# The expert part's GpSimd sums given to VectorE, two more rows fetched ahead of the optional slots, and the last operands moved behind a guard

## The chip, the cores and the metric

The kernel runs on one core of one Trainium2 chip, as one launch. The metric is the device time of a run in microseconds (us); the time before is the median of three runs. The engines are named as the profile names them: PE is TensorE's matmul, PEld its weight load, DVE is VectorE, ACT is ScalarE, POOL is GpSimd, SP is SyncE. An engine with a "q" behind it (ACTq, POOLq) is that engine's instruction queue: branches, semaphore work and DMA issues.

## The reference, cut to what matters

```
attn_out = attention(x, state)              # 8 batches
x = rearranged to 4352 tokens of 512        # 34 tiles of 128 tokens
e_idx = argmax(x @ w_gate)                  # one of 8 experts a token
for e in range(8):
    mask = e_idx == e
    h = maximum(x[mask] @ w1[e], 0)         # 512 -> 1024
    out[mask] = gate_w[mask] * eom[mask, e] * (h @ w2[e])
h = out @ w_in                              # 512 -> 2048, float64 weights
g = h * clip(h + 3, 0, 6) / 6
result = g @ w_out                          # 2048 -> 512, float64 weights
```

## The kernel before, in words

Every fp32 product is made of three: each operand is kept as a high part (a copy rounded to the type fp32r, cast by ACT) and a low part (the subtraction, on DVE or POOL), and PE adds high·high, low·high and high·low. So whatever PE multiplies has first passed ACT and then a subtraction.

The program has three stretches. Until about 107 us of the span it computes the attention and the routing. Then comes the **expert part** (functions `early` and `moe1`, to about 614 us). The tokens, sorted by expert, are dealt to 41 slots of 128 rows; where an expert's last slot isn't full it is padded, so the number of slots that hold tokens depends on the data. Slots 19 to 25 are optional (`OPT`): all work of such a slot stands behind a guard (`guard`, L1299 in the profile), a branch on a register that every engine takes for itself. In this run slots 19 to 22 are computed and 23 to 25 skipped. Last comes the second part (`moe2`, from 614 us), six blocks of eight `unit`s each, matmuls of 384 columns and their activations.

What slot t does: `gather` fetches its 128 rows by an indirect DMA on POOL's queue, after `column` has fetched their row numbers (`ci`); `slot_T` transposes them on PE and splits them (`xh` by ACT, `xl` by DVE); `slot_M1` is 24 matmuls of 512 columns against the first weights `w00h`/`w00l` in the order xh·w00h, xl·w00h, xh·w00l for each half of the columns, with the relu on ACT; `slot_TH` transposes the result and splits it (`hh` by ACT, `hl` by DVE); `slot_M2` is 24 matmuls against `w01h`/`w01l` in the order hh·w01h, hl·w01h, hh·w01l; ACT scales the result and it is stored in `ys_dram`.

The loop of `moe1` orders them in iteration t as: column t+5, gather t+3, M1 of t, T of t+1, `weights` of t+1 for the first matrix, one or two conversion pieces, M2 of t-1, TH of t, `weights` of t for the second matrix. Three helpers in it matter here.

- `weights` (L735): when a flag of slot t says that a new expert begins, four pieces of 128x1024 are split: ACT casts the high part (L703), and the low part (L709) is subtracted by DVE in pieces 0, 2 and 3 and by POOL in piece 1. Behind the branch SP fetches the raw weights of the expert after that (L726) into the tile that was just split.
- `convert` (32 pieces in iterations 2 to 18 and 26 to 36, two of them in 29, 31, 33 and 35) turns float64 words of the second part's weights into fp32: seven DVE operations (L924 to L931) and one POOL addition (L933, tile `quad`). `parts` then splits them (tile `st`, L944 on ACT, L945 on DVE) and SP writes them to DRAM.
- The rows of slot 26 (`OPT.stop`), the first one behind the optional slots, are fetched and transposed early, in iterations 13 and 14 (`HOIST`), into tiles of their own.

At the seam between expert part and second part, iteration 40 also builds the operands `X` of the second part's first block (`block_operands`, seven steps `ops[0]` to `ops[6]`; the splits are L1044 on ACT and L1045 on DVE, two sums L1053 on DVE). The last slot's M2 isn't done in the loop: `last_M2` (L1070) cuts it into three parts of 8 matmuls, which stand in the gaps of the first `unit`, behind its first two products (L1116, 12 matmuls), its third and fourth, and its fifth.

The expert part is laid out by a schedule that is fixed when the program is built: each engine has one list of instructions and works through it in order, with waits on semaphores ("waits Pool_49" is a wait on POOL's counter).

Of the kernel before, what the change touches and what calls it, by code (L numbers as in the profile page):

```python
# [9 lines left out]
F32 = mybir.dt.float32  # L10
# [4 lines left out]
ALU = mybir.AluOpType  # L15
# [5 lines left out]
P = 128  # L21
B, H, S, NS, D = 8, 8, 512, 32, 64
NT = B * (S + NS)
DM = H * D
# [3 lines left out]
OPT = range(19, 19 + SLOTS - TILES)  # L28
# [667 lines left out]
def split(k, which, i, eng):  # L696
    high(k, which, i)
    low(k, which, i, eng)


def high(k, which, i, copy=None):
    c = slice(1024 * i, 1024 * i + 1024)
    (copy or k.nc.scalar.copy)(k.W[0][which][0][:, c], k.raw[which].rearrange("p a b -> p (a b)")[:, c])  # L703


def low(k, which, i, eng):
    hi, lo = k.W[0][which]
    c = slice(1024 * i, 1024 * i + 1024)
    eng.tensor_tensor(out=lo[:, c], in0=k.raw[which].rearrange("p a b -> p (a b)")[:, c], in1=hi[:, c], op=ALU.subtract)  # L709
# [8 lines left out]
def fetch(k, t, which):  # L718

    nc = k.nc  # L720
    raw, queue = k.raw[which], nc.sync
    if t not in k.lregs:
        fetch_flags(k, t)
    nd, ev = k.lregs[t]
    src = (k.w1_d, k.w2_d)[which]
    queue.dma_start(out=raw, in_=src[bass.ds(ev, 1)].rearrange("o (k p) f -> p (o k) f", p=P), cond=nd)  # L726


def weights(k, t, which):
    if t == SLOTS:  # L730
        return
    if t not in k.regs:
        k.regs[t] = k.nc.values_load(k.tab[0:1, 0, t:t + 1], engines=[ET.Activation, ET.DVE, ET.Pool], min_val=0,
                                     max_val=1)
    with k.tc.If(k.regs[t] == 1):  # L735
        for i in range(4):
            split(k, which, i, k.nc.gpsimd if i == 1 else k.nc.vector)
    if t < SLOTS - 1:
        fetch(k, t, which)

# [9 lines left out]
def guard(k, t):  # L750
    if t not in OPT or t in k.inside:
        return nullcontext()
    return k.tc.If(k.vregs[t] == 1)


def column(k, t):
    if t >= SLOTS or t in k.ci:
        return
    nc = k.nc
    queue, engine = (nc.sync, ET.SP) if t < EARLY + 5 else (nc.gpsimd, ET.Pool)  # L760
    col = nc.values_load(k.cols[0:1, t:t + 1], engines=[engine], min_val=0, max_val=511)
    own = "o" * (t == OPT.stop)
    ci = k.tb.tile([P, 4], I32, tag="ci" + own, name="ci", bufs=1 if own else 8)
    queue.dma_start(out=ci, in_=k.inv_d.rearrange("(p c) o -> p c o", p=P)[:, bass.ds(col, 1), :].rearrange("p c o -> p (c o)"))
    k.ci[t] = ci


def gather(k, t):
    if t >= SLOTS or t in k.xg or t in k.xT:
        return  # L770
    x = k.xgp.tile([P, DM + 1], F32, tag="xg", name="xg", bufs=4)
    ins = k.nc.gpsimd.indirect_dma_start(
        out=x[:, 0:DM], out_offset=None, in_=k.xs[0:P * EARLY_TILES] if t < EARLY else k.xs,
        in_offset=bass.IndirectOffsetOnAxis(ap=k.ci[t][:, 0:1], axis=0))
    if t < EARLY:
        k.tc.keep_in_program_order(ins)
    k.xg[t] = x
# [125 lines left out]
def convert_load(k, i):  # L903
    if i >= NCONV:
        return
    r, c = convert_place(i)
    d = k.cv.tile([P, CW, 2], I32, tag="d", name="d", bufs=2)
    src = (k.win_d if i < NCONV // 2 else k.wout_d).bitcast(I32)
    k.nc.gpsimd.dma_start(out=d.rearrange("p a b -> p (a b)"), in_=src[r:r + P, 2 * c:2 * c + 2 * CW])
    k.cvd[i] = d  # L910


def convert(k, i):
    if i >= NCONV:
        return
    nc = k.nc
    v = nc.vector
    d = k.cvd.pop(i)
    if i % 4 == 0:
        k.quad = k.cv.tile([P, 4, CW], F32, tag="quad", name="quad", bufs=2)  # L920
    hw, lw = d[:, :, 1], d[:, :, 0]
    e = k.wk.tile([P, 2, CW], I32, tag="e", name="e", bufs=1)[:, 0]
    base = float(896 << 20)
    v.tensor_scalar(out=e, in0=hw, scalar1=0x7FF00000, scalar2=None, op0=ALU.bitwise_and)  # L924
    v.tensor_scalar(out=e, in0=e, scalar1=base, scalar2=float(1151 << 20), op0=ALU.max, op1=ALU.min)
    v.tensor_scalar(out=e, in0=e, scalar1=base, scalar2=8.0, op0=ALU.subtract, op1=ALU.mult)
    v.scalar_tensor_tensor(out=e, in0=hw, scalar=-0x80000000, in1=e, op0=ALU.bitwise_and, op1=ALU.bitwise_or)
    v.tensor_scalar(out=hw, in0=hw, scalar1=3, scalar2=0x7FFFF8, op0=ALU.logical_shift_left, op1=ALU.bitwise_and)
    v.tensor_tensor(out=hw, in0=hw, in1=e, op=ALU.bitwise_or)
    f = e.bitcast(F32)  # L930
    v.scalar_tensor_tensor(out=f, in0=lw.bitcast(mybir.dt.uint32), scalar=2.0 ** -52, in1=f, op0=ALU.mult, op1=ALU.mult)  # L931
    w = k.quad[:, i % 4, :]
    nc.gpsimd.tensor_tensor(out=w, in0=f, in1=hw.bitcast(F32), op=ALU.add)  # L933
    if i >= NCONV // 2:
        k.tasks.append(lambda f=i - NCONV // 2: out_part(k, f, w))
    elif i % 4 == 3:
        k.tasks += in_sums(k, i // 4, k.quad)
# [11 lines left out]
def out_part(k, f, w):  # L949

    st = parts(k, w, (2, CW))
    k.nc.sync.dma_start(out=k.wdn[f], in_=st.rearrange("p h c -> p (h c)"))
# [314 lines left out]


FLAGS, HOIST = -6, OPT.start - 6
PIECES = sorted([t for t in range(2, 37) if t not in OPT] + [29, 31, 33, 35])  # L1270


def moe1(k):
    k.tasks = []
    k.cv = k.xb = k.tc.alloc_tile_pool(name="conv", bufs=1, reuse_waits="tile")
    convert_load(k, 0)
    convert_load(k, 1)
    i = 0

    def piece(n=2):  # L1280
        nonlocal i
        for _ in range(min(n, len(k.tasks))):
            k.tasks.pop(0)()
        convert(k, i)
        convert_load(k, i + 2)
        i += 1

    for t in range(2, SLOTS):
        if t - FLAGS in [*OPT, OPT.stop]:
            flags(k, t - FLAGS)  # L1290
        if t == OPT.start:
            k.fixed = {}
        if t == HOIST:
            column(k, OPT.stop)
            gather(k, OPT.stop)
        column(k, t + 5)
        gather(k, t + 3)
        within = t in OPT and t - 1 in OPT
        with guard(k, t - 1) if within else nullcontext():  # L1299
            if within:  # L1300
                k.inside = (t - 1,)
            if t > EARLY:
                start_y(k, t - 1)
            slot_M1(k, t)
            if t + 1 < SLOTS and t + 1 != OPT.stop:
                slot_T(k, t + 1)
            if t == 39:
                for j in (2, 3):
                    block_T(k, k.blocks[0], j, ("y2", "y3")[j % 2])
            if t == 38:  # L1310
                for j in (0, 1):
                    block_T(k, k.blocks[0], j, ("y2", "y3")[j % 2])
                for j in (2, 3, 4):
                    block_gather(k, k.blocks[0], j)
            if t == 40:
                fetch_down(k, 0, 0)
                for f in ops[0:3]:
                    f()
            weights(k, t + 1, 0)
            if t == 39:  # L1320
                k.ring.fetch()
            for _ in range(PIECES.count(t)):
                piece()
            if t == PIECES[-1] + 1:
                piece(6)
            if t > EARLY:
                slot_M2(k, t - 1)
            if t == 39:
                block_gather(k, k.blocks[0], 5)
                block_T(k, k.blocks[0], 4, "y2")  # L1330
            if t == 40:
                ops[3]()
            slot_TH(k, t)
            if t == 40:
                for f in ops[4:]:
                    f()
            if t == 39:
                block_T(k, k.blocks[0], 5, "y3")
                ops = block_operands(k, k.blocks[0])
            if t == HOIST + 1:  # L1340
                slot_T(k, OPT.stop)
            weights(k, t, 1)
        k.inside = ()
        if t + 1 == OPT.stop:
            k.fixed = None
        if 4 <= t < 11:
            row_table(k, 5 * (t - 4))
        if t == 37:
            assert i >= NCONV and not k.tasks
            k.cv.release()  # L1350
            k.reg = k.tc.alloc_tile_pool(name="region", bufs=1, reuse_waits="tile")
            k.blocks = [Block(k, g) for g in range(len(HALVES))]
            k.ring = Ring(k, 8 * len(k.blocks))
            for j in (0, 1):
                block_gather(k, k.blocks[0], j)
        if t == 40:
            k.ring.fetch()
# [84 lines left out]
```

## Time and profile before

| | us |
|---|---|
| median of three runs | 1372.44 (1371.67 to 1373.47) |
| the profiled execution | 1371.76 |
| its span | 1370.2 |
| PE busy in the span | 1319.0 (96%) |
| DVE, ACT, POOL busy | 796.7 (58%), 564.5 (41%), 286.1 (21%) |
| granted TensorE clock, mean | 0.985 of full speed |

The span runs from the profiled execution's first instruction to its last; its time is 1.56 us longer. All places below are given in us from the span's start. In a timeline an entry can stand for several instructions of one kind (the x behind it), its us run from the first one's start to the last one's end, and in brackets stands how long the engine was idle before it and what released it. "issue" is a wait that nothing in the profile explains.

### The profile page before, as it was taken

Reading aid. Unit: us, or ns where it says so; the run is one execution under the profiler, and the core shown is the slowest. Engines: PE = TensorE matmul, PEld = TensorE weight load, DVE = VectorE, ACT = ScalarE, POOL = GpSimd, SP = SyncE. Lnnn points to the kernel's source line nnn. Section 1 sums busy time; section 2 is a strip of 40 time slices with the busy share of each in tenths; the row PEclk is TensorE's granted clock in tenths of the full one; section 3 lists DMA queues with packets and bytes.
Section 4 is the critical chain, followed back from the end, with each engine's and each line's share of the span. In section 5 each row is a group of like instructions: output and inputs, shape, how many; then the busy total and the mean of one; then the engine's idle time right before and its main releaser. Section 6 shows DMA issues by size and latency. Waiting matters only on the chain.

```text
span 1370.2 us, 20252 instructions
## 1 busy us (share of the span) xinstructions
PE 1319.0 (96%) x7091; PEld 1119.1 (82%) x7091; DVE 796.7 (58%) x1525; ACT 564.5 (41%) x1021; POOL 286.1 (21%) x290
## 2 busy tenths in 40 slices
PE   8977999999997999998999999999999999999996
PEld 6766888888775788877989898889898988888885
DVE  7987588877725776435446445644564465445442
ACT  5753344453533433343334433443353344333432
POOL 2346333343423343210000200020010001000101
PEclk9999999999998999999999999999999999999998
DMA  9964768867642554346553433353333334333540
GB/s 352 362 207 141 237 211 266 253 197 233 223 158 94 201 172 160 125 161 231 207 205 110 169 123 123 111 182 146 138 138 147 124 115 156 123 135 117 200 169 32
DMA packets 84289, 238.22 MB, mean 174 GB/s; under 512 B 9104, under 2 KB 24592, under 8 KB 84048
## 3 DMA queue, kind: packets, MB, share of 16 engines
q1 hardware_dynamic: 56896, 168.46, 35.1%
q0 software_dynamic: 15824, 46.57, 10.7%
q10 hardware_dynamic: 11456, 21.78, 4.3%
q8 instruction: 58, 0.95, 0.3%
q14 instruction: 55, 0.45, 0.1%
HBM read 312.98 MB, written 54.09 MB: 268 GB/s over the span
## 4 chain that ended last, share of the span: by engine, by line
PE 47%; issue 6%; ACT 1%; DVE 0%; POOL 0%; POOLq 0%; ACTq 0%
PE ch L1116 22%; PE acc L1087 8%; PE acc L1089 8%; PE acc L1088 8%; PE xTp L1030 1%; PE yp L1070 0%; POOL out_dram L1101 0%; ACT o L1100 0%; DVE r L1132 0%; ACT g L1136 0%; ACT r L1128 0%; DVE g L1139 0%; POOLq L1429 0%; DVE s L1169 0%; DVE s L1183 0%
## 5 line engine op out<-in xcount | busy, mean ns | idle before, releaser
L1116 PE MATMUL ch<-X,wr 128*128 128x384 f32 (+1 forms) x2016 | 367.8, 329 | 0.8 <-DVE oid L1027 0.8
L1116 PEld LDWEIGHTS ch<-X,wr 128*128 128x128 f32 x2016 | 342.5, 188 | 20.7 <-DVE s L1183 2.4
L1139 DVE TENSOR_TENSOR g<-r,g 128x384 fp32r<-128x384 f32 (+1 forms) x192 | 103.0, 537 | 84.7 <-ACT g L1136 79.1
L1136 ACT CAST g<-r 128x384 fp32r<-128x384 f32 (+1 forms) x192 | 95.1, 495 | 135.2 <-DVE r L1132 104.5
L1128 ACT ACTIVATE r<-s,three 128x384 f32<-128x384 f32 (+1 forms) x144 | 86.4, 600 | 139.5 <-DVE s L1169 115.5
L1132 DVE SCALAR_TENSOR_TENSOR r<-r,s 128x384 f32<-128x384 f32 (+1 forms) x144 | 77.3, 537 | 73.0 <-ACT r L1128 71.8
L1101 POOL DMA_INDIRECT out_dram<-o,oid x34 | 33.5, 986 | 382.3 <-ACT o L1100 374.3
L1014 POOL DMA_INDIRECT xg<-ys_dram,rowi x34 | 39.1, 1151 | 340.9 <-DVE oid L1027 250.7
L1087 PE MATMUL acc<-w01h,g 128*128 128x512 f32 x272 | 110.1, 405 | 0.0
L1087 PE MATMUL acc<-w00h,g 128*128 128x512 f32 x272 | 107.7, 396 | 0.7 <-ACT o L1100 0.7
L1089 PE MATMUL acc<-w00h,g 128*128 128x512 f32 x272 | 108.1, 397 | 0.0
L1088 PE MATMUL acc<-w00l,g 128*128 128x512 f32 x272 | 107.3, 394 | 0.0
L1089 PE MATMUL acc<-w01h,g 128*128 128x512 f32 x272 | 107.2, 394 | 0.0
L1088 PE MATMUL acc<-w01l,g 128*128 128x512 f32 x272 | 107.2, 394 | 0.0
L1132 DVE SCALAR_TENSOR_TENSOR r<-r,ch 128x384 f32<-128x384 f32 (+1 forms) x48 | 25.6, 532 | 120.5 <-ACT r L1128 120.5
L834 ACT ACTIVATE h<-hp 128x512 f32<-128x512 f32 x76 | 45.0, 599 | 121.8 <-PE hp L802 119.1
L802 PE MATMUL hp<-w00h,xh 128*128 128x512 f32 x304 | 90.0, 418 | 5.0 <-ACTq L1299 2.0
L802 PE MATMUL hp<-w00l,xh 128*128 128x512 f32 x304 | 86.3, 404 | 6.8 <-POOL w00l L709 4.9
L1128 ACT ACTIVATE r<-ch,three 128x384 f32<-128x384 f32 (+1 forms) x48 | 27.1, 564 | 154.2 <-PE ch L1116 154.2
L802 PE MATMUL hp<-w00h,xl 128*128 128x512 f32 x304 | 85.9, 406 | 0.0
L802 PE MATMUL yp<-w01h,hh 128*128 128x512 f32 x296 | 78.4, 406 | 1.4 <-ACTq L735 1.0
L802 PEld LDWEIGHTS hp<-w00l,xh 128*128 128x128 f32 x304 | 58.1, 192 | 23.1 <-POOL w00l L709 5.7
(224 smaller groups left out, 2251.0 us busy)
## 6 DMA issues: line engine op xcount, KB each, us to landing
raw<-in_w_dram SPq DMA_DIRECT2D x75, 2048.0 KB
wr<-wup_dram SPq DMA_DIRECT2D x48, 1792.0 KB
wup_dram<-st SPq DMA_DIRECT2D x28, 512.0 KB
ys_dram<-y ACTq DMA_DIRECT2D x41, 256.5 KB
xt<-in_xt_dram SPq DMA_DIRECT2D x8, 1040.0 KB
xT<-in_xT_dram SPq DMA_DIRECT2D x16, 512.0 KB
xs_dram<-row ACTq DMA_DIRECT2D x8, 1024.0 KB
d<-in_win_dram POOLq DMA_DIRECT2D x16, 512.0 KB, 5.4
```

Of the source, the lines that this page charges most:

```text
L802: nc.tensor.matmul(out, a, b, start=(i == 0), stop=(i == len(parts) - 1))
L834: nc.scalar.activation(h[:, 512 * f:512 * f + 512], ps[f], AF.Relu)
L1014: k.nc.gpsimd.indirect_dma_start(out=x, out_offset=None, in_=k.ys[0:P * min(T + 8, SLOTS)], in_offset=bass.IndirectOffsetOnAxis(ap=k.rowi[ ...
L1087: nc.tensor.matmul(a, g[:, 0, t], wh[:, c], start=not late and u == 0, stop=False)
L1088: nc.tensor.matmul(a, g[:, 0, t], wl[:, c], start=False, stop=False)
L1089: nc.tensor.matmul(a, g[:, 1, t], wh[:, c], start=False, stop=bool(late) and u == 7)
L1101: ins = nc.gpsimd.indirect_dma_start(out=k.out, out_offset=bass.IndirectOffsetOnAxis(ap=b.ids[j], axis=0), in_=o, in_offset=None).ins
L1116: nc.tensor.matmul(ps[:, 0:W], w[:, d, i, hw, :], b.X[i][:, hx, d, :], start=start and n == 0, stop=n == 5, skip_group_check=True)
L1128: nc.scalar.activation(rs[kind], h, AF.Relu, bias=k.three)
L1132: v.scalar_tensor_tensor(out=rs[kind], in0=rs[kind], scalar=6.0, in1=h, op0=ALU.min, op1=ALU.mult)
L1136: nc.scalar.copy(k.gs[kind][:, 0], rs[kind])
L1139: v.tensor_tensor(out=k.gs[kind][:, 1], in0=rs[kind], in1=k.gs[kind][:, 0], op=ALU.subtract)
```

## The change

- `weights`: the subtraction of piece 1 goes from POOL to DVE.
- `convert`: the last addition goes from POOL to DVE.
- `HOISTS`: slots 27 and 28 get their row numbers and rows early too, in iterations 14 and 15, in tiles of their own (`xgo27`, `xgo28`). Their transposes stay where they were.
- Iteration 40: `ops[4:]`, which are the split of X[3], the two sums and the splits of X[4] and X[2], are emitted behind `weights(k, 40, 1)` instead of ahead of it. The flag of slot 40 is not set in this run.

```diff
@@ def weights(k, t, which):
     with k.tc.If(k.regs[t] == 1):
         for i in range(4):
-            split(k, which, i, k.nc.gpsimd if i == 1 else k.nc.vector)
+            split(k, which, i, k.nc.vector)
@@ def column(k, t):
-    own = "o" * (t == OPT.stop)
+    own = f"o{t}" if t in HOISTS else ""
     ci = k.tb.tile([P, 4], I32, tag="ci" + own, name="ci", bufs=1 if own else 8)
@@ def gather(k, t):
-    x = k.xgp.tile([P, DM + 1], F32, tag="xg", name="xg", bufs=4)
+    if t in HOISTS[1:]:
+        x = k.cv.tile([P, DM], F32, tag=f"xgo{t}", name="xg", bufs=1)
+    else:
+        x = k.xgp.tile([P, DM + 1], F32, tag="xg", name="xg", bufs=4)
@@ def convert(k, i):
     w = k.quad[:, i % 4, :]
-    nc.gpsimd.tensor_tensor(out=w, in0=f, in1=hw.bitcast(F32), op=ALU.add)
+    v.tensor_tensor(out=w, in0=f, in1=hw.bitcast(F32), op=ALU.add)
@@
+HOISTS = [OPT.stop, OPT.stop + 1, OPT.stop + 2]
@@ def moe1(k):
-        if t == HOIST:
-            column(k, OPT.stop)
-            gather(k, OPT.stop)
+        if HOIST <= t < HOIST + 3:
+            column(k, HOISTS[t - HOIST])
+            gather(k, HOISTS[t - HOIST])
@@
             slot_TH(k, t)
-            if t == 40:
-                for f in ops[4:]:
-                    f()
             if t == 39:
                 block_T(k, k.blocks[0], 5, "y3")
                 ops = block_operands(k, k.blocks[0])
             if t == HOIST + 1:
                 slot_T(k, OPT.stop)
             weights(k, t, 1)
+            if t == 40:
+                for f in ops[4:]:
+                    f()
```

Line numbers of the changed kernel are 3 higher than before around L709 to L930 and 4 higher from L1299 on; the name of a row tells it in any case.

**Place 1** is PE's list where the skipped optional slots end and slot 26's M1 begins (`w00l` is the low part of the first weights). Before:

```order
L1299 UNCONDITIONAL_BRANCH
L1299 UNCONDITIONAL_BRANCH [waits PE_49]
L802 MATMUL hp<-w00h,xh 128x512 [waits Activation_49] x4
L802 MATMUL hp<-w00h,xl 128x512 x4
L802 MATMUL hp<-w00l,xh 128x512 [waits DVE_49]
L802 MATMUL hp<-w00l,xh 128x512 [waits Pool_49]
L802 MATMUL hp<-w00l,xh 128x512 [waits DVE_49] x2
L802 MATMUL hp<-w00h,xh 128x512 x4
```

Changed:

```order
L1303 UNCONDITIONAL_BRANCH
L1303 UNCONDITIONAL_BRANCH [waits PE_49]
L805 MATMUL hp<-w00h,xh 128x512 [waits Activation_49] x4
L805 MATMUL hp<-w00h,xl 128x512 x4
L805 MATMUL hp<-w00l,xh 128x512 [waits DVE_49] x4
L805 MATMUL hp<-w00h,xh 128x512 x4
```

The wait on POOL's counter is gone; all four low pieces are waited for on DVE's.

**Place 2** is DVE's list at the first conversion, with the split of the hidden values (`hl`) behind it. Before:

```order
L929 TENSOR_TENSOR d<-d,e 128x512 [waits DVE_49]
L931 SCALAR_TENSOR_TENSOR e<-d,e 128x512 [waits DVE_49]
L853 TENSOR_TENSOR hl<-tp,hh 128x512 [waits Activation_49] x2
L735 COMPARE_AND_BRANCH
L709 TENSOR_TENSOR w01l<-raw_67,w01h 128x1024 [waits DMAHW1_49,Activation_49]
L709 TENSOR_TENSOR w01l<-raw_67,w01h 128x1024 [waits Activation_49] x2
```

Changed:

```order
L932 TENSOR_TENSOR d<-d,e 128x512 [waits DVE_49]
L934 SCALAR_TENSOR_TENSOR e<-d,e 128x512 [waits DVE_49]
L936 TENSOR_TENSOR quad<-e,d 128x512 [waits DMAHW3_49,DMAHW2_49,DVE_49]
L856 TENSOR_TENSOR hl<-tp,hh 128x512 [waits Activation_49] x2
L735 COMPARE_AND_BRANCH
L709 TENSOR_TENSOR w01l<-raw_67,w01h 128x1024 [waits DMAHW1_49,Activation_49]
L709 TENSOR_TENSOR w01l<-raw_67,w01h 128x1024 [waits Activation_49] x3
```

The addition stands between the last integer operation and `hl`, and a split of weights has four DVE pieces in a row instead of three.

**Place 3** is DVE's list at the seam to the second part, from the last slot's `hl` on (`X` are operands of the first block, `s_8388` the sum of the unit's second product, `r` and `ch` belong to its first activation). Before:

```order
L853 TENSOR_TENSOR hl<-tp,hh 128x512 [waits Activation_49] x2
L1045 TENSOR_TENSOR X<-xraw,X 128x768 [waits DMAHW1_49,Activation_49]
L1053 TENSOR_TENSOR xraw<-xraw,s_8256 128x2x384 [waits DVE_49] x2
L1156 TENSOR_TENSOR s_8388<-ch,s_8387 128x384 [waits DMAHW0_49,PE_49,Activation_49]
L1045 TENSOR_TENSOR X<-xraw,X 128x768 [waits DMAHW0_49,Activation_49]
L1045 TENSOR_TENSOR X<-xraw,X 128x768 [waits DMAHW4_49,Activation_49]
L735 COMPARE_AND_BRANCH
```

Changed:

```order
L856 TENSOR_TENSOR hl<-tp,hh 128x512 [waits Activation_49] x2
L735 COMPARE_AND_BRANCH
L709 TENSOR_TENSOR w01l<-raw_67,w01h 128x1024 [waits DMAHW0_49,Activation_49]
L709 TENSOR_TENSOR w01l<-raw_67,w01h 128x1024 [waits Activation_49] x3
L735 UNCONDITIONAL_BRANCH
L735 UNCONDITIONAL_BRANCH [waits DVE_49]
L1159 TENSOR_TENSOR s_8388<-ch,s_8387 128x384 [waits DMAHW0_49,PE_49,Activation_49]
L1048 TENSOR_TENSOR X<-xraw,X 128x768 [waits DMAHW1_49,Activation_49]
L1056 TENSOR_TENSOR xraw<-xraw,s_8256 128x2x384 [waits DVE_49] x2
L1135 SCALAR_TENSOR_TENSOR r<-r,ch 128x384 [waits Activation_49]
L1048 TENSOR_TENSOR X<-xraw,X 128x768 [waits DMAHW0_49,Activation_49]
L1048 TENSOR_TENSOR X<-xraw,X 128x768 [waits DMAHW4_49,Activation_49]
```

The guard stands directly behind `hl` now, the unit's sum comes ahead of the X splits, and one step of the activation (L1135) stands among them. ACT's list changes in the same way: the copy of the unit's first product comes directly ahead of the guard, and the casts of X[3], X[4] and X[2] behind it.

## Rows read from the trace of the kernel before

**Rows 1.** The page, part 1: busy us, share of the span, instructions of each engine.

```profile
PE 1319.0 (96%) x7091; PEld 1119.1 (82%) x7091; DVE 796.7 (58%) x1525; ACT 564.5 (41%) x1021; POOL 286.1 (21%) x290
```

**Rows 2.** Windows: stretch, its us, busy of PE, PEld, DVE, ACT, POOL, granted clock, DMA share, GB/s.

```profile
140.00:630.00 490.00, 471.86 (x2220) 381.97 (x2219) 316.76 (x528) 203.30 (x324) 165.00 (x174) 0.98 0.58 190
415.00:425.00 10.00, 7.99 (x18) 5.83 (x19) 0.15 (x1) 0.60 (x1) 3.33 (x6) 0.50 0.21 56
```

**Rows 3.** Waits, all engines: who waited for whom, us in total, times, longest.

```profile
PE yp L1070 <- ACTq L735: 5.6, 1, 5.6
PE hp L802 <- POOL w00l L709: 4.9, 2, 2.9
...
PE yp L802 <- DVE hl L853: 0.9, 1, 0.9
```

**Rows 4.** Timeline, 360 to 370 us, DVE and PE.

```profile
362.87 3.51 DVE L709 TENSOR_TENSOR w00l<-raw,w00h 128x1024 fp32r<-128x1024 f32 x3
...
368.66 0.97 PE L802 MATMUL hp<-w00l,xh 128*128 128x512 f32 x3 [2.00 <-POOL w00l L709]
```

**Rows 5.** Timeline, 412 to 430 us, PE at slot 26's first product.

```profile
415.58 1.22 PE L802 MATMUL hp<-w00h,xh 128*128 128x512 f32 x2 [1.09 <-issue]
...
420.36 1.65 PE L802 MATMUL hp<-w00l,xh 128*128 128x512 f32 x3 [1.43 <-POOLq L1299]
...
426.11 0.60 PE L815 MATMUL xTp<-ident,xg 128*128 128x128 f32 x4
```

**Rows 6.** Timeline, 440 to 452 us, slot 27's first product.

```profile
442.33 0.39 PE L802 MATMUL hp<-w00l,xh 128*128 128x512 f32 x1
442.76 3.31 DVE L927 SCALAR_TENSOR_TENSOR e<-d,e 128x512 int32<-128x512 int32 x1
443.17 2.35 POOL L709 TENSOR_TENSOR w00l<-raw,w00h 128x1024 fp32r<-128x1024 f32 x1
...
445.57 1.65 PE L802 MATMUL hp<-w00l,xh 128*128 128x512 f32 x3 [2.86 <-POOL w00l L709]
...
447.91 1.28 DVE L853 TENSOR_TENSOR hl<-tp,hh 128x512 fp32r<-128x512 f32 x2
...
450.73 0.60 PE L815 MATMUL xTp<-ident,xg 128*128 128x128 f32 x4
```

**Rows 7.** Timeline, 612 to 635 us, the seam to the second part.

```profile
615.00 1.28 DVE L853 TENSOR_TENSOR hl<-tp,hh 128x512 fp32r<-128x512 f32 x2
615.56 0.49 ACT L1154 COPY s<-ch 128x384 f32<-128x384 f32 x1
...
618.05 1.70 ACT L1044 CAST X<-xraw 128x768 fp32r<-128x768 f32 x2 [2.00 <-DVE xraw L1053]
...
619.27 1.81 DVE L1045 TENSOR_TENSOR X<-xraw,X 128x768 fp32r<-128x768 f32 x2
...
619.85 3.59 PE L1070 MATMUL yp<-w01h,hh 128*128 128x512 f32 x8 [5.60 <-ACTq L735]
...
625.39 2.03 PE L1070 MATMUL yp<-w01l,hh 128*128 128x512 f32 x8
...
627.26 2.27 PE L1116 MATMUL ch<-X,wr 128*128 128x384 f32 x12
```

**Rows 8.** Line L709: durations of one in ns (min/median/max), first and last start, forms.

```profile
L709 DVE TENSOR_TENSOR w00l<-raw,w00h x21: 1210/1220/4050, 95.5 to 439.0; 128x1024 fp32r<-128x1024 f32 x21
...
L709 POOL TENSOR_TENSOR w00l<-raw,w00h x7: 2352/2458/2500, 93.7 to 443.2; 128x1024 fp32r<-128x1024 f32 x7
```

**Rows 9.** Lines, DVE by form: count, busy us, mean ns of one, idle before.

```profile
L1132 DVE SCALAR_TENSOR_TENSOR r<-r,s 128x384 f32<-128x384 f32 x120 | 67.0, 559 | 62.1 <-ACT r L1128 61.1
L929 DVE TENSOR_TENSOR d<-d,e 128x512 int32<-128x512 int32 x32 | 22.2, 693 | 1.1
```

**Rows 10.** Timeline, 154 to 161 us, the tightest conversion.

```profile
156.44 1.28 DVE L853 TENSOR_TENSOR hl<-tp,hh 128x512 fp32r<-128x512 f32 x2
...
157.18 1.69 PEld L802 LDWEIGHTS yp<-w01h,hl 128*128 128x128 f32 x8 [0.51 <-DVE hl L853]
```

## The prediction

> **What bounds the kernel now.** I read the page's busy shares first, then the list of waits, then the timeline around each wait that ended PE's idle time. PE is busy for 96% of the span [rows 1], so a change of the other engines can win only what PE idles, and what its lower clock costs behind a pause. In the 490 us from 140 to 630 us, the stretch in which the change acts, PE is busy 471.86 us; 18.1 us is all its idle time. DVE is busy 316.76 us there, 65%, and POOL 165.00 [rows 2]. The waits say where the 18.1 us lie: 5.6 us in one piece at the seam, where PE waits for ACT to pass the guard L735, and 4.9 us in two pieces, where PE waits for POOL's low piece of the weights [rows 3]. The timelines add 1.43 us on POOL's way past the skipped slots [rows 5], and what a pause does to the clock: the stretch 415 to 425 us shows the granted clock at 0.50, that is 1.2 of 2.4 GHz [rows 2]. A row of eight 512-column matmuls takes 625.39 to 627.26, which is 0.234 us each at full clock, and 3.59 us, 0.45 each, behind the wait at 619.85 [rows 7].
>
> **The change part by part.** *(a) Weights at 366 us.* PE came to its low matmuls at 366.66 and waited 2.00 us, to 368.66, for POOL's piece [rows 4]. A DVE piece is 1.22 us by the median, a POOL piece 2.46 [rows 8]; three DVE pieces take 3.51 us [rows 4], so 1.15 of pitch, and four end at 362.87 + 4 x 1.15 + 0.06 = 367.53. PE, unstopped from 366.66, wants the fourth at 366.66 + 2 x 0.234 = 367.13. It waits 0.40 in place of 2.00: **gain 1.6** (1.2 to 2.4; below if the pieces run a third slower, above if the next raw weights, which load when the last subtraction is done, arrive earlier).
>
> *(b) Slot 26 behind the skipped slots.* The wait of 1.43 on POOL goes [rows 5]; DVE's count is reached, since the neighbouring piece of DVE let PE through before POOL did. From 415.58 to 426.11 PE does 22 matmuls in 10.53 us [rows 5], at full clock 22 x 0.234 = 5.15. So the gain lies between 1.43 (clock stays low) and 5.38 (full at once). The wait marked "issue", 1.09, ahead of it stays [rows 5], so part of the low clock has a cause that is not removed: I take the middle, **3.4**.
>
> *(c) Slot 27.* PE's first low matmul ends at 442.33 + 0.39 = 442.72; it waits 2.86 for POOL's piece, and the remaining 15 matmuls end at 450.73, 8.01 us later, in place of 15 x 0.234 = 3.51 [rows 6]. **Gain 4.5** (2.86 to 4.6). While POOL subtracts, DVE's L927 takes 3.31 us [rows 6], though its neighbour of the same size, L929, has a mean of 0.693 [rows 9]; without POOL's piece that 2.6 us is back, which pays for DVE's fourth piece (1.15) and the addition (0.69). DVE's `hl`, at 447.91 before [rows 6], comes about 0.8 earlier, PE 4.5 earlier; it still lies ahead of its use, barely.
>
> The other ten POOL pieces ended no wait of PE [rows 3]; DVE's work instead of them is paid for in the same way, since a DVE piece at its side is held too (maximum 4.05 against a median of 1.22 [rows 8]). I cost them at nothing; if that cover failed, each could cost up to 1.15.
>
> *(d) The additions.* 32 more DVE operations of 0.69 (the nearest row is L929, same size [rows 9]) make 22 us, in DVE's idle 35%. Each stands ahead of `hl`. The first is the tightest: `hl` was late already, PE's weight load waited 0.51 for it at 157.18 [rows 10], so it loses 0.7. In the others that I followed in the timeline, `hl` is done before PE turns to it, mostly by more than 0.69. The one place where PE waited 0.9 for `hl` [rows 3] lies behind an iteration in which DVE itself waited for POOL's addition, which took longer than DVE's will; it gets shorter by some 0.3. **Loss 0.4** (0 to 4, the upper end being six such places at 0.69).
>
> *(e) The seam.* Before, PE waited 5.60 us, from 614.25 to 619.85, because ACT had to cast X[4] and X[2] (ended 618.05 + 1.70 = 619.75) ahead of the guard [rows 7]. Changed, ACT's copy of the unit's first product is the last thing ahead of it. It ended at 615.56 + 0.49 = 616.05 behind a cast of X[3]; without that cast I put it at 615.4, and the guard at 0.1 (619.75 to 619.85). PE then does 8 matmuls (1.87), two products (623.28 to 625.39, 2.11), 8 more (1.87) [rows 7]: 615.5 + 5.85 = 621.35. Now DVE comes last: `hl` ends at 615.00 + 1.28 = 616.28, and from there to 619.27 + 1.81 = 621.08 six operations took 4.8 us [rows 7]. Changed: 616.28 + 0.2 for the guard (twice ACT's) + 4.8 + 0.56 for the activation's step, which now stands among them (L1132 [rows 9]), + 0.56 for the sum behind it = 622.4. The next pair of products starts there instead of at 627.26: **gain 4.8**. Ends: 5.9, if DVE is not what PE waits for (621.35); 2.3, if a guard costs 1.09 (the "issue" row [rows 5]) and the two casts' 1.70 lie in series with DVE: 616.28 + 1.09 + 4.8 + 1.12 + 1.70 = 625.0.
>
> For a branch a row shows 0.1 (ACT, 619.85) and up to 1.09 (PE, 415.58). The Trainium skill (Runtime: NRT & Kernel Launch, Instruction fetch mechanics) says that a taken branch to a target outside the loaded window has to fetch its instructions before execution goes on; by that rule the seam's guard, which is jumped over in this run, would cost nearer to 1.09 on DVE, and the gain of (e) would be 3.9, towards R1 below. No row shows such a fetch there.
>
> *The hoist.* The rows of slots 27 and 28 ended no wait of PE; the early fetches are two more short issues on POOL's queue in a stretch where nothing waits for POOL. **0**.
>
> Sum: 1.6 + 3.4 + 4.5 - 0.4 + 4.8 = **13.9 us**. Against the profiled execution's 1371.76 that is 1357.9; the median of the runs is 0.68 higher, so **1358.5**.
>
> **The rivals.** *R1, a new wait at the seam:* the moved operands come later than PE wants them, and the gain of (e) is 2.3, not 4.8: 1361.0. For it: six DVE operations and two casts pile up behind one guard; against: DVE stands idle afterwards. *R2, the skipped slots keep PE slow:* another engine's way past the guards takes POOL's place, (b) gives nothing: 1361.9; both together 1364.4. For it: PE waits for ACT and for "issue" right before.
>
> *R3, slower: VectorE becomes the one that ends last.* Every `hl` comes 0.69 late and PE waits for it: 32 x 0.69 = 22.1 us lost against the 14.3 of (a), (b), (c) and (e), that is 1372.44 + 7.8 = 1380.2. It decides when `hl` has less than 0.69 us to spare in over 24 of the 32 conversions ((14.3 + 2.7) / 0.69). For it: the row at 157.18; against: DVE's 65%, and POOL no longer holds it. The Trainium skill speaks for this rival (Perfetto Trace Analysis, Optimizing Scalar/DVE Operations): it would move work away from a saturated DVE, to GpSimd too, though it adds that the two share a read port of SBUF. At 65% the trace does not show saturation.
>
> *R4, no change:* each removed wait is replaced by one on DVE's piece as long: 1372.4.
>
> **How the numbers follow.** Forecast 0.62, R1 0.17, R2 0.11, R3 0.06, R4 0.04. A measurement tells 0.2%, 2.7 us, from no change; so faster 0.90 (forecast, R1, R2), same 0.04 (R4), slower 0.06 (R3). The ends: all low values give 1.2 + 1.4 + 2.9 + 2.3 - 4 = 3.8, that is 1368.6; all high ones 2.4 + 5.4 + 4.6 + 5.9 = 18.3, that is 1354.1, and the 0.9 us at `hl` and a tenth at each of the ten swaps that I cost at nothing, whose raw weights load earlier, could go too: 1352.2. That all are low at once is unlikely: the range is **1352 to 1367**, which takes in the forecast, R1 and R2 with most of their bounds and leaves out R3 and R4.
>
> **What would show it.** Right: no wait of PE on POOL's `w00l`; slot 26's M1 shorter by about 3 us; PE's last M2 at the seam starting 1 to 1.5 us after the TH, and its next pair of products near 622.4 less what was won before it; DVE near 68 to 70% in the stretch. Wrong: PE's waits on `hl` growing from 0.9 us to 5 or more (d, R3), a wait of PE on DVE's X or sum at the seam of over 3 us (R1), the clock between slots 25 and 27 as low as before (R2).

## The result and the profile after

The changed kernel takes 1355.49 us (median of four, 1352.62 to 1358.56) against 1372.06 for the kernel before beside it: ratio 0.9878, 95% interval [0.9849, 0.9907], 16.6 us less at the medians. The forecast was 1358.5 in a range of 1352 to 1367. The profiled execution took 1357.82 us, 13.9 less than that of before; it lies in the upper half of the four runs. Two executions at a far lower granted clock, one of the kernel before (2418 us at 0.82) and one with the hoist put back (2163 us at 0.56), are left out of every comparison below.

The page, part 1, of the changed kernel, and the two windows that answer to [rows 2] (the same columns; the first ends at 617 us, since the seam comes earlier):

```profile
PE 1314.4 (97%) x7091; PEld 1117.6 (82%) x7091; DVE 809.7 (60%) x1569; ACT 564.2 (42%) x1021; POOL 211.0 (16%) x246
```

```profile
140.00:617.00 477.00, 465.26 (x2215) 377.56 (x2214) 329.51 (x571) 202.47 (x324) 92.41 (x130) 0.99 0.61 196
413.50:423.50 10.00, 8.01 (x28) 5.99 (x28) 0.15 (x1) 0.91 (x2) 2.00 (x4) 0.83 0.10 31
```

DVE's busy share of the stretch went from 65 to 69% (329.51 of 477), and PE's idle time in it from 18.1 us to 11.7 (477 - 465.26). In the ten us at slot 26 PE did 28 matmuls in place of 18, at a granted clock of 0.83 in place of 0.50; but the two windows do not lie alike to the start of the slot. From the slot's first matmul to the transposes behind it, before and changed, the windows are:

```profile
413.76:426.11 12.35, 9.83 (x24) 6.95 (x25) 0.15 (x1) 0.60 (x1) 4.61 (x6) 0.59 0.24 67
414.26:422.99 8.73, 7.49 (x24) 5.63 (x25) 0.15 (x1) 0.60 (x1) 1.23 (x3) 0.80 0.11 33
```

So the slot's first product is 3.6 us shorter, at a clock of 0.80 in place of 0.59.

PE's longest waits in the changed kernel from 140 to 640 us (who waited for whom, us in total, times, longest):

```profile
PE yp L805 <- ACT w01h L703: 2.9, 3, 2.5
PE hp L805 <- ACTq L1303: 2.0, 1, 2.0
PE yp L805 <- DVE hl L856: 1.9, 2, 1.6
PE hp L805 <- issue: 1.2, 1, 1.2
PE yp L1073 <- ACTq L735: 1.2, 1, 1.2
PE ch L1119 <- DVE s L1166: 1.0, 1, 1.0
```

The two largest waits of before [rows 3] are gone or small: none on POOL's pieces is left, and 1.2 us of 5.6 at the seam. But the first row, PE's wait of 2.9 us for the cast of `w01h`, was 0.2 us before.

To see where the time went, take PE instructions that both kernels have and compare their starts. Timeline of the changed kernel, PE, at such places:

```profile
361.89 1.31 PE L805 MATMUL hp<-w00h,xh 128*128 128x512 f32 x4
...
363.98 1.41 PE L805 MATMUL hp<-w00l,xh 128*128 128x512 f32 x4
...
368.03 0.60 PE L818 MATMUL xTp<-ident,xg 128*128 128x128 f32 x4
...
380.52 0.60 PE L818 MATMUL xTp<-ident,xg 128*128 128x128 f32 x4
...
383.57 0.73 PE L805 MATMUL yp<-w01h,hh 128*128 128x512 f32 x2 [2.46 <-ACT w01h L703]
...
387.44 2.81 PE L805 MATMUL yp<-w01h,hl 128*128 128x512 f32 x8
...
416.23 1.04 PE L805 MATMUL hp<-w00h,xh 128*128 128x512 f32 x2 [1.24 <-issue]
...
422.99 0.60 PE L818 MATMUL xTp<-ident,xg 128*128 128x128 f32 x4
...
442.28 1.10 PE L805 MATMUL hp<-w00l,xh 128*128 128x512 f32 x4
...
443.22 0.60 PE L818 MATMUL xTp<-ident,xg 128*128 128x128 f32 x4
...
614.92 2.35 PE L1119 MATMUL ch<-X,wr 128*128 128x384 f32 x12 [1.02 <-DVE s L1166]
```

The same instructions of before started at these times (four of them are not in the rows above the prediction):

```profile
363.88 0.94 PE L802 MATMUL hp<-w00h,xh 128*128 128x512 f32 x3
...
372.28 0.60 PE L815 MATMUL xTp<-ident,xg 128*128 128x128 f32 x4
...
384.82 0.60 PE L815 MATMUL xTp<-ident,xg 128*128 128x128 f32 x4
...
387.63 2.04 PE L802 MATMUL yp<-w01h,hl 128*128 128x512 f32 x8
```

| place | before | changed | changed is ahead by | step |
|---|---|---|---|---|
| first product at 364 us | 363.88 | 361.89 | 2.0 | |
| transposes behind it | 372.28 | 368.03 | 4.3 | **(a)** +2.3 |
| transposes of the next slot | 384.82 | 380.52 | 4.3 | 0 |
| hl·w01h of that iteration | 387.63 | 387.44 | 0.2 | **-4.1** |
| slot 26, behind "issue" | 415.58 | 416.23 | -0.7 | -0.8 |
| transposes behind it [rows 5] | 426.11 | 422.99 | 3.1 | **(b)** +3.8 |
| transposes behind slot 27 [rows 6] | 450.73 | 443.22 | 7.5 | **(c)** +4.4 |
| second pair of products of the unit [rows 7] | 627.26 | 614.92 | 12.3 | **(e)** +4.8 |

The steps (b), (c) and (e) are there, near their forecast sizes; (a) is there and is given back 15 us later, by a wait that the prediction did not have.

The 2.0 us at the first place are, for the larger part, a wait that rows 3 do not show: in the kernel before, PE waited for the rows of an early slot.

```profile
135.72 0.66 PE L815 MATMUL xTp<-ident,xg 128*128 128x128 f32 x4 [2.68 <-DMA xg<-xs_dram,ci]
```

The changed kernel was 2.1 us behind at 130 us and 0.6 ahead at 136. This wait comes ahead of the first conversion (155 us), and it does not go with the edits: the changed kernel with its raw weights in quarters (below) has it in one of two profiles (2.7 us) and not in the other, and the kernel before with quarters is without it.

### The profile page after: what moved, and what is told of

The parts are those of the page before. It is cut to its first block, busy times and chain, and to the rows that moved or that the text cites. A ratio compares the mean times of both kernels' runs of the same rounds, so it can differ in the third digit from the quotient of the medians.

```text
span 1356.3 us, 20116 instructions
## 1 busy us (share of the span) xinstructions
PE 1314.4 (97%) x7091; PEld 1117.6 (82%) x7091; DVE 809.7 (60%) x1569; ACT 564.2 (42%) x1021; POOL 211.0 (16%) x246
## 4 chain that ended last, share of the span: by engine, by line
PE 47%; issue 6%; DVE 1%; ACT 1%; POOL 0%; POOLq 0%; ACTq 0%; DVEq 0%
PE ch L1119 22%; PE acc L1092 8%; PE acc L1090 8%; PE acc L1091 8%; PE xTp L1033 1%; POOL out_dram L1104 0%; ACT o L1103 0%; DVE X L1048 0%; DVE r L1135 0%; ACT g L1139 0%; ACT r L1131 0%; DVE g L1142 0%; DVE xraw L1056 0%; POOLq L1433 0%; DVE s L1172 0%
## 5 line engine op out<-in xcount | busy, mean ns | idle before, releaser
L1135 DVE SCALAR_TENSOR_TENSOR r<-r,s 128x384 f32<-128x384 f32 (+1 forms) x144 | 77.2, 536 | 73.0 <-ACT r L1131 71.8
L1135 DVE SCALAR_TENSOR_TENSOR r<-r,ch 128x384 f32<-128x384 f32 (+1 forms) x48 | 25.5, 532 | 115.7 <-ACT r L1131 115.7
L805 PE MATMUL yp<-w01h,hl 128*128 128x512 f32 x296 | 76.3, 400 | 2.0 <-DVE hl L856 1.9
```

The lines of the kernel that those rows point to most:

```text
L805: nc.tensor.matmul(out, a, b, start=(i == 0), stop=(i == len(parts) - 1))
L1135: v.scalar_tensor_tensor(out=rs[kind], in0=rs[kind], scalar=6.0, in1=h, op0=ALU.min, op1=ALU.mult)
```

## The experiments

The verdicts are ratios to the kernel before on the same chip. The three experiments ran on three chips, so times of different experiments are not compared.

**1. The changed kernel again, and three of its edits one at a time.** The four runs of the changed kernel lay in two groups, so it ran once more beside the single edits, on another chip.

> The changed kernel once more, because its four runs lie in two groups, 1352.6 to 1353.2 and 1357.8 to 1358.6, and its profile is of the upper group. In that profile PE gains about 2.2 us at 364 us (no wait for POOL's low piece) and gives back 4.5 us at 383 to 387 us, where the cast of w01h waits for its raw weights. Theory L (a race of a transfer with PE): runs fall into the same two groups again, some 5 us apart, and a profile of the lower group has no wait of over 1 us for w01h near 383 us. Rival: the two groups come from the attention part or from elsewhere, and a profile of the lower group keeps the wait.

Weights alone:

```diff
-            split(k, which, i, k.nc.gpsimd if i == 1 else k.nc.vector)
+            split(k, which, i, k.nc.vector)
```

> The kernel before with one edit: piece 1 of the weights' subtraction on DVE; the conversions' additions stay on POOL, no further rows are hoisted, the seam is as before. Theory (each wait on POOL's weights is one of the removed ones, and the edits act apart): about 7.4 us of gain behind slot 26 and 27 (2.8 and 4.6), the 2.2 at 364 us kept or given back by the raw weights' wait: 1362 to 1365 against 1372. Rival: without the additions moved too, POOL is still late somewhere and the gain is under 4 us.

The seam alone:

```diff
             slot_TH(k, t)
-            if t == 40:
-                for f in ops[4:]:
-                    f()
...
             weights(k, t, 1)
+            if t == 40:
+                for f in ops[4:]:
+                    f()
```

> The kernel before with one edit: the last operands emitted behind the guard of slot 40's second weights. Theory: the 5.6 us wait of PE on ACT at the seam falls to about 1.2 us, gain 5 to 6 us: 1366 to 1367 against 1372. Rival: the seam's gain in the changed kernel came in part from VectorE being earlier there, and alone it is under 3 us.

The additions alone:

```diff
-    nc.gpsimd.tensor_tensor(out=w, in0=f, in1=hw.bitcast(F32), op=ALU.add)
+    v.tensor_tensor(out=w, in0=f, in1=hw.bitcast(F32), op=ALU.add)
```

> The kernel before with one edit: the conversions' last addition on DVE instead of POOL. Theory: no change or a loss of up to 1 us, 1372 to 1373, with PE's waits on the low part of the hidden values at 1 to 2 us in all. Rival 1: DVE's 22 us more make the low parts late, PE's waits on them grow to 4 us or more, 1376 and up. Rival 2: POOL's queue is freed for its gathers and weights' pieces, and the time falls by 2 us or more.

| kernel | ratio to before | 95% interval | us against 1387.89 |
|---|---|---|---|
| changed, again | 0.9887 | [0.9872, 0.9901] | -15.7 |
| weights alone | 0.9939 | [0.9926, 0.9951] | -8.5 |
| seam alone | 0.9964 | [0.9951, 0.9977] | -5.0 |
| additions alone | 1.0011 | [1.0002, 1.0021] | +1.5 |

(The us are the ratio times 1387.89.) Both gains came out as the theory had them; DVE's additions are a small loss by themselves, a little over the 1 us of the theory, and not a gain by a freed POOL; PE's waits on `hl` are 2.6 us in that profile, where 1 to 2 were expected. In the seam's run PE's wait is 1.16 us, as in the whole, while the weights and additions are as before, so that gain is the move's own. Timeline of the seam-alone kernel, PE:

```profile
632.25 2.14 PE L1070 MATMUL yp<-w01h,hh 128*128 128x512 f32 x8 [1.16 <-ACTq L735]
```

The repeat's profile is 12 us longer than the first, yet not at this place: its wait list has 0.6 us for `w01h` in place of 2.9, and between 380 and 400 us it makes up 3.6 us of the way. The 15 us it lost before lie in the attention and routing, ahead of 139 us, and all four profiles of this chip have them. The three single edits' profiles, by contrast, all hold the wait for `w01h` (2.4, 2.0 and 2.1 us in all). The four runs of the repeat did not fall into two groups, though that was expected (1369.96 to 1372.05); the ten of the seam alone did (five from 1379.73 to 1381.47, five from 1384.22 to 1386.57). So the wait differs from one execution to the next, and kernels with part of the change have it as well. That the two groups are the executions with and without it is not shown: each kernel has one profile.

**2. The wait for the raw weights, the additions and the hoist, on one chip.** Control:

> The changed kernel as the control of the three others on the same chip. Every theory: 0.985 to 0.989 of the kernel before.

Raw weights in four transfers, one a piece, each of which can start when its own piece is subtracted:

```diff
-    queue.dma_start(out=raw, in_=src[bass.ds(ev, 1)].rearrange("o (k p) f -> p (o k) f", p=P), cond=nd)
+    ks = raw.shape[1] // 4
+    for j in range(4):
+        sl = slice(ks * j, ks * j + ks)
+        queue.dma_start(out=raw[:, sl], in_=src[bass.ds(ev, 1)].rearrange("o (k p) f -> p (o k) f", p=P)[:, sl], cond=nd)
```

> The changed kernel with the raw weights of the next expert fetched as four transfers of a quarter each, one for each piece, so that a quarter is on its way when its own subtraction is done and not when the last one is. Theory L (the landing of the raw weights of the second matrix near 383 us decides whether PE idles 0 or 2.5 us there, and its clock falls for some microseconds behind it): the landing comes up to 3.5 us earlier (three DVE pieces of 1.15), PE's wait for w01h falls under 0.7 us in the profile, and the time is 0 to 5 us under the control, with runs closer together: about 3 us at the median. Rival (the memory's rate sets the landing, whenever the transfers begin): the landing stays, no change against the control.

The changed kernel with the addition as before:

```diff
-    v.tensor_tensor(out=w, in0=f, in1=hw.bitcast(F32), op=ALU.add)
+    nc.gpsimd.tensor_tensor(out=w, in0=f, in1=hw.bitcast(F32), op=ALU.add)
```

> The changed kernel with the conversions' addition back on POOL, all else as changed. Theory A (the additions alone cost 1 to 3 us, as their run without the other edits showed, because they stand ahead of the low part of the hidden values, and that is so in the changed kernel too): 1 to 3 us under the control. Rival B (with the weights' pieces off POOL, DVE has the time back and the additions cost nothing; moving them back makes ACT's casts wait for POOL again): equal to the control or above it by up to 2 us.

The changed kernel with only slot 26 hoisted:

```diff
-HOISTS = [OPT.stop, OPT.stop + 1, OPT.stop + 2]
+HOISTS = [OPT.stop]
...
-        if HOIST <= t < HOIST + 3:
+        if HOIST <= t < HOIST + 1:
```

> The changed kernel with the rows of slots 27 and 28 fetched at their old places again, all else as changed. Theory (no wait of PE ended on these rows): within 1.5 us of the control. Rival H (the sum of the three single edits, about 12 us, falls short of the whole's 15 to 16, and the hoist makes the rest: with POOL's queue behind the skipped slots held by these fetches, slots 26 to 28 lose time): 3 us or more above the control, with a wait of PE for rows or on POOL's queue between 410 and 435 us.

| kernel | ratio to before | 95% interval | runs, us |
|---|---|---|---|
| changed, control | 0.9880 | [0.9853, 0.9906] | 1351.94 to 1359.35 |
| raw weights in quarters | 0.9860 | [0.9838, 0.9881] | 1349.58 to 1353.99 |
| additions back | 0.9872 | [0.9850, 0.9893] | 1352.13 to 1357.98 |
| hoist back | 0.9890 | [0.9863, 0.9916] | 1354.02 to 1361.48 |

The intervals overlap; by time alone none of the three differs from the control. The profiles tell more. Timeline of the control, ACT's cast that PE waits for and DVE's subtractions that free the raw tile before it:

```profile
365.89 4.62 DVE L709 TENSOR_TENSOR w01l<-raw,w01h 128x1024 fp32r<-128x1024 f32 x4
...
379.53 3.89 ACT L703 CAST w01h<-raw 128x1024 fp32r<-128x1024 f32 x4 [3.68 <-DMA raw<-in_w_dram]
```

The same in the changed kernel's first profile:

```profile
365.96 4.62 DVE L709 TENSOR_TENSOR w01l<-raw,w01h 128x1024 fp32r<-128x1024 f32 x4
...
382.48 3.89 ACT L703 CAST w01h<-raw 128x1024 fp32r<-128x1024 f32 x4 [6.57 <-DMA raw<-in_w_dram]
```

And with the raw weights in quarters:

```profile
363.19 4.62 DVE L709 TENSOR_TENSOR w01l<-raw,w01h 128x1024 fp32r<-128x1024 f32 x4
...
373.09 3.91 ACT L703 CAST w01h<-raw 128x1024 fp32r<-128x1024 f32 x4
```

The same program frees the tile at 370.51 and 370.58 and starts to use its next weights 9.0 and 11.9 us later: 3 us of difference in the landing of one tile from DRAM, from one execution to another. PE is at its matmuls near 381 us in both. In the one it waits 0.4 us in all, in the other 2.9. Matched matmul by matmul, the two profiles are 3.6 us apart behind this place, of 3.7 at the end. With quarters the cast starts 5.3 us behind the last subtraction, and waits for no transfer. What moved in between shows in the DMA view of the six us from 365 to 371 (queue: packets, MB, share of 16 engines; q1 has the raw weights, q0 the gathers, q10 a store of `ys_dram`). The changed kernel's first profile:

```profile
q1 hardware_dynamic: 186, 0.76, 57.3%
q0 software_dynamic: 177, 0.47, 20.5%
q10 hardware_dynamic: 144, 0.26, 11.5%
```

The control:

```profile
q1 hardware_dynamic: 343, 1.40, 72.7%
q0 software_dynamic: 65, 0.24, 9.9%
q10 hardware_dynamic: 33, 0.05, 2.8%
```

With quarters, and below it the six us from 362.3, which lie to the subtraction (2.7 us earlier here) as 365 to 371 do in the other two:

```profile
q1 hardware_dynamic: 750, 2.07, 90.5%
```

```profile
q1 hardware_dynamic: 445, 1.64, 74.8%
```

Two raw tiles, 4.2 MB, are fetched one behind the other here, for both matrices, and in the next six us q1 is busy throughout in the first profile:

```profile
q1 hardware_dynamic: 849, 2.37, 101.3%
```

That is 0.4 MB a us. So the 0.64 MB that the first profile moved less in the six us are 1.6 us of the 3; the other queues moved 0.73 MB in them, against 0.29 in the control. Where the rest comes from stays open. The rival had a point: from 371 us on the rate sets the landing. Quarters win for two reasons that this test does not take apart: the transfers begin with the first piece (they are issued at 364.54, 365.66, 366.79 and 367.92, one behind each subtraction, where the control issues its one at 370.64), and the first cast reads one quarter and not the whole tile. This is the wait that took back the gain of (a). That PE loses 4.1 us for waits of 2.9 in place of 0.2 goes with the clock: the last four hh·w01h matmuls, from 385.47 to 387.44, ran at a granted clock of 0.57. The eight hl·w01h matmuls behind them took 2.81 us, against 2.04 in before's, and these are the 0.8 of the next step. The spread of the runs was 4.4 us with quarters and 7.4 without, the median 2.4 us lower where 3 were expected; that quarters gain time in the changed kernel is likely by this, and not shown clear of noise.

**3. The same questions without that wait.** Where no run has the wait, small differences show better; so the additions and the hoist were put back in the kernel with quarters, and the quarters put into the kernel before.

> The changed kernel with the raw weights fetched in quarters, again, as the control of the next two: 0.984 to 0.988 of the kernel before, its runs within 3 us of each other, since no run has the wait for w01h near 383 us.

> The control with the conversions' addition back on POOL. Theory A (the additions cost 1 to 3 us in the changed kernel, as PE's waits on the low part of the hidden values, 2.0 us with them and 0.4 without): 1 to 3.5 us under the control, the fastest version so far. Rival B (they cost nothing): within 1 us of the control.

> The control with the rows of slots 27 and 28 fetched at their old places. Theory: within 1 us of the control, no new wait between 405 and 435 us. Rival H: 2 us or more above the control.

> The kernel before with the raw weights fetched in quarters, no other edit. Theory L (the wait for the raw weights near 385 us is in the kernel before too, in some of its executions; the whole change only makes PE come to it 2 us sooner): 0 to 4 us under the kernel before, with PE's wait for w01h under 0.5 us. Rival (the change made that wait): no difference.

| kernel | ratio to before | 95% interval | median, us |
|---|---|---|---|
| changed, quarters | 0.9862 | [0.9842, 0.9881] | 1354.09 |
| the same, additions back | 0.9824 | [0.9803, 0.9845] | 1349.81 |
| the same, hoist back | 0.9864 | [0.9844, 0.9884] | 1354.78 |
| before, quarters | 0.9991 | [0.9975, 1.0008] | 1369.78 |

**The hoist** is worth nothing here: 0.9862 and 0.9864, as costed (0.9880 and 0.9890 in experiment 2, inside the noise). **The additions** cost 4.3 us at the medians, over the 3.5 that were expected at most, though the two intervals touch. Where they cost it can be seen at one place. Timeline of the changed kernel, PE, at a double conversion:

```profile
472.43 1.90 PE L805 MATMUL yp<-w01h,hl 128*128 128x512 f32 x7 [1.61 <-DVE hl L856]
```

With the additions back on POOL (and the raw weights in one transfer), the same place:

```profile
466.65 2.13 PE L805 MATMUL yp<-w01h,hl 128*128 128x512 f32 x8 [0.43 <-DVE hl L856]
```

That is 1.2 us, and the same two waits of the quarters' pair are 1.69 and 0.51. Matched matmul by matmul, the two profiles of the pair are 4.8 us apart, but 1.9 of these are there at 140 us, ahead of the first conversion: the one with the additions on DVE holds the wait for gathered rows at 136 us (2.7 us), the other does not. Behind that 2.9 us are left, 1.2 of them at this row and a wait on `xl` of 0.65 at 308 us as the next. So the additions do cost, in the same direction three times (1.5 us alone by the ratio, 1.8 and 4.3 at the medians in experiment 2 and here, the 1.8 inside the noise); the 4.3 can be too large. The kernel with the weights on DVE, the seam moved, the raw weights in quarters and the additions left on POOL has the lowest ratio of all: 1349.81 us, with an interval wholly below 1 and below that of the changed kernel ([0.9803, 0.9845] against [0.9853, 0.9906] for the control of experiment 2).

**Quarters in the kernel before** make no difference that can be measured, where 0 to 4 us were expected. The test isn't clean: in its profile the waits on POOL's pieces are 7.0 us in three places, where the kernel before has 4.9 in two. Whether the raw weights hold up the kernel before in some of its executions stays open; that they hold up each single edit's in the profile is shown above.

## Why the prediction held

- **The bound.** Right: PE's waits and the clock behind them. The four places give 2.3 + 3.8 + 4.4 + 4.8 = 15.3 us; 4.9 of these are given back between 380 and 416 us, and 2.0 were there ahead of 364, which makes the 12.3 at the seam. Another 1.6 come in behind it, without a row of their own. In the control of experiment 2 the same four steps are 2.4, 3.8, 4.4 and 4.8 us, and only 1.3 are given back. So the steps repeat; but that the first profile's whole, 13.9 us, equals the forecast sum to the tenth is **luck**: what was not foreseen (4.9 lost, 3.6 come in from elsewhere, 1.0 more at the four places) happens to cancel.
- **(a) Weights at 366 us:** forecast 1.6, came 2.3. The four low matmuls took 1.41 us (at 363.98), 0.3 more than the 1.10 of the four at 442.28 in the same product of slot 27, so the wait on DVE's fourth piece is near the 0.4 worked out; the short wait for the cast of `w00h` ahead of them went too. But in this execution it was **given back** at 383 us, and this is what the prediction lacks: of the next raw weights it said only that they load earlier. How long two such transfers take, one behind the other, was not asked. In the profile of before PE came to that place later, and waited 0.2 us for them.
- **(b) Slot 26:** forecast 3.4 as the middle between a clock that stays low and one that is full at once; came 3.8. The clock from the slot's first matmul to the transposes was 0.80, between the 0.59 of before and full. The waits on ACT and on "issue" stayed, at 2.0 and 1.2.
- **(c) Slot 27:** forecast 4.5, came 4.4. The cover was right as well: without POOL's piece L927 (now L930) has a mean of 0.693 us over all 32, where before one of them took 3.31 [rows 6].
- **The other pieces at nothing:** right, with room to spare. Lines of DVE by form, changed kernel:

```profile
L709 DVE TENSOR_TENSOR w01l<-raw,w01h 128x1024 fp32r<-128x1024 f32 x28 | 32.4, 1216 | 7.0 <-ACT w01h L703 6.8
L709 DVE TENSOR_TENSOR w00l<-raw,w00h 128x1024 fp32r<-128x1024 f32 x27 | 31.9, 1236 | 1.6 <-ACT w00h L703 1.6
L930 DVE SCALAR_TENSOR_TENSOR e<-d,e 128x512 int32<-128x512 int32 x32 | 22.2, 693 | 1.1
L936 DVE TENSOR_TENSOR quad<-e,d 128x512 f32<-128x512 f32 x32 | 22.2, 692 | 1.1
```

  In the kernel before, the same view has 22 and 21 such pieces:

```profile
L709 DVE TENSOR_TENSOR w01l<-raw,w01h 128x1024 fp32r<-128x1024 f32 x22 | 36.6, 1700 | 6.4 <-ACT w01h L703 6.0
L709 DVE TENSOR_TENSOR w00l<-raw,w00h 128x1024 fp32r<-128x1024 f32 x21 | 32.7, 1585 | 4.2 <-ACT w00h L703 4.2
```

  So 55 pieces take 64.3 us where 43 took 69.3: DVE does twelve more and is done sooner. With the weights alone changed it is 64.7.
- **(d) The additions:** the price of one, 0.69, is exact (L936, 692 ns). Their cost was put at 0.4 with an upper end of 4. Measured: 1.5 us alone (0.3 to 2.9 by the interval), 4.3 at the medians in the quarters' pair, 2.9 in that pair's profiles behind 140 us. The first conversion cost less than the 0.7 put down: PE waits 0.27 us there. The step that failed is the one on the place where PE waited 0.9 for `hl`: it was to get shorter, because DVE no longer waits for POOL's addition, and it grew to 1.6. At a double conversion two additions stand ahead of one `hl`, and PE comes 7 us earlier than before by (b) and (c), so the old margin says little. With PE as early and the additions on POOL the wait is 0.43, so it is the additions that make it.
- **(e) The seam:** forecast 4.8, came 4.8. PE's last M2 started 1.2 us behind its idle point, DVE was last again, and the pair of products waited 1.0 us for the sum s (L1166), as the chain of operations had it. The guard on DVE cost 0.24. The Trainium skill (Runtime: NRT & Kernel Launch, Instruction fetch mechanics) says that a taken branch stops for a fetch when its target lies outside the loaded window. Whether the target of this guard does, no row shows; it jumps over four subtractions only, and by its 0.24 us no such stop is seen here.
- **The hoist:** forecast 0, measured 0.
- **The rivals.** R1 fell (the wait at the seam is 1.0 and was in the sum). R2 fell (b gave 3.8). R4 fell. R3, VectorE as the one that ends last, fell as a whole, though it has a small part in it: the additions do cost, at a DVE share of 69%. The Trainium skill (Perfetto Trace Analysis, Optimizing Scalar/DVE Operations) would move work off a saturated DVE, but adds that moving it to GpSimd might not help, since the two share a read port of SBUF. The weights' pieces are as that caution has it; the additions were better on GpSimd, though DVE at 69% is not saturated. That the port is what holds DVE's pieces, no run here shows.
- **What stays open.** The three single edits sum to -12.0 us where the whole is -15.7 on the same chip. The hoist does not make the rest (1.4 and 0.3 us by the ratios of its two tests, inside the noise). The profiles of the single edits hold the wait for the raw weights, 2.0 to 2.4 us each, and the whole's on that chip only 0.6, which is enough for it, but that is argued from one profile each. Nor is it shown why the wait for gathered rows at 136 us comes in one execution and not in another.

The forecast is 3 us above the median that came. The profiled execution met it, and two of the four runs were some 5 us faster; the control's profile, 3.7 us faster than the first and without most of the wait for the raw weights, suggests that these two were without it, but no profile of them exists.

## What to carry to other kernels

When a wait is taken away, ask how long the next transfer behind it takes, not only when it can start: the removed wait may have hidden it, and a transfer that begins piece by piece as its tile comes free can take that risk away: in none of the five profiles with quarters does PE wait for `w01h`. Two operations that move together for the same reason need not be worth the same: the weights' pieces on GpSimd slowed VectorE (its busy time in the whole fell from 796.7 to 789.0 us with twelve more of them) and were better on VectorE. The additions hardly did (it rose from 796.7 to 817.6, by nearly all of 32 x 0.69) and were better left on GpSimd. A step that is emitted behind a guard instead of ahead of it can win nearly as much as moving work between engines (5.0 us here, 8.5 for the weights' pieces), and what it costs can be worked out from the row of operations that then comes last.

## What the runs showed of the hardware

- Raw weights whose tile came free at the same moment (370.51 and 370.58 us) were used 9.0 us later in one execution and 11.9 in another of the same program; in the six us in which it was busy throughout the queue moved 2.37 MB, 0.4 a us.
- A GpSimd subtraction beside VectorE's costs VectorE more than itself: twelve pieces of 1.22 us were added to VectorE, and its time on these lines fell by 5.0 us (4.6 with nothing else changed).
- One chip needed some 15 us more for the stretch up to 139 us in all four profiles taken there, and about the same time as the others from then on.
